# Infini-attention beside a SiLU feed-forward on one core: the bias of the turned heads made by VectorE, GpSimd's small scale operations planned at their real length, two buffers for memory's sums

## The chip, the core and the metric

The kernel runs on one core of one Trainium2 chip. The metric is the device time of one execution in microseconds, here the median of several runs; less is better. A core has five engines that run side by side, each with its own queue of instructions that it takes strictly in order: TensorE (PE in the profile, with its weight loads as PEld), VectorE (DVE), ScalarE (ACT), GpSimd (POOL) and SyncE (SP), which here issues most of the transfers. [...]

## The reference

The input has 2048 rows of 448 numbers. One branch is an attention with memory: 16 heads of 28, four segments of 512 rows; inside a segment a causal softmax attention, and beside it a retrieval from a matrix that sums the keys and values of all earlier segments. The other branch is a feed-forward layer, 448 to 1792 to 448, with SiLU. A gate mixes the two row by row.

```python
for s in range(N):                                   # 4 segments
    logits = jnp.einsum("bhqd,bhkd->bhqk", qs, ks) * scale + mask
    p = _softmax(logits, axis=-1)
    a_dot = jnp.einsum("bhqk,bhkd->bhqd", p, vs)
    pq = phi(qs)                                     # phi(t) = t + 1 if t > 0 else exp(t)
    num = jnp.einsum("bhld,bhde->bhle", pq, M)
    den = jnp.einsum("bhld,bhd->bhl", pq, z)[..., None] + 1e-6
    o = g * (num / den) + (1.0 - g) * a_dot
    pk = phi(ks)
    M = M + jnp.einsum("bhld,bhle->bhde", pk, vs)
    z = z + jnp.einsum("bhld->bhd", pk)
...
h = _silu(jnp.einsum("bsd,df->bsf", x, w1))
out = jnp.einsum("bsf,fd->bsd", h, w2)
return g * a + (1 - g) * b                           # g = sigmoid(x . gate_w)
```

## The kernel before

**Precision.** Almost every product is made of float16 pairs: an operand is split in a high part (made by ScalarE as a scaled copy) and the rest (made by VectorE or GpSimd), and TensorE multiplies high by high, high by low and low by high. The power-of-two scales for this are found on the chip from the sizes of the data. A few columns hold them (`top`, `up`), and GpSimd makes from them, in many operations on one to sixteen numbers per partition, every scale and bias that later instructions take as an operand. The helper `by` (L533, L535) issues these, in the functions `true`, `kscale`, `others` and `derive`.

**Stages.** In the first 180 us or so the projections run (`project`): x and the weights are loaded, split, multiplied to q, k, v and the gate (`product`, L637), and q, k and v are written to scratch memory in DRAM. In the same stage `memory` adds up phi(k) times v per segment and group of four heads: TensorE leaves the sum in PSUM, VectorE folds it into a buffer `md` (L1065), GpSimd masks it with `bds` (L1068) and adds it to `macc` (L1070), ScalarE and GpSimd split it again (L1073, L1074), and `retrieve` multiplies it with phi(q) (L1091 to L1106). From about 180 to 455 us the attention runs: 16 tiles (4 segments by 4 groups), each of four heads, between them the first pass of the feed-forward layer (10 of its 14 slices of 128) and part of the second. After that the second pass ends, with the output projection (`sc<-wos,oT`).

**Two kinds of heads.** Three of four heads of a tile (all four of the first tile) are computed with the keys along the partitions: their row maxima are found ahead of time in `maxima` (L744, L754), enter the product as two more rows, and ScalarE only takes exp (L1385). The fourth head of tiles 1 to 15, the *turned* one, has the queries along the partitions (`scores`, L1331 to L1345). Its four blocks of rows come in three groups, block 3 (512 wide), blocks 2 and 0 (384 and 128), block 1 (256). For each group TensorE multiplies (L1331), VectorE finds the maximum of each row in PSUM with the mask added (L1337; each block is one reduction and one short read of the accumulator), ScalarE turns each maximum into a bias, maximum times a scale plus a constant (L1341, the function `drop`), and takes exp with that bias (L1345). For every head ScalarE then makes the high half `phl` (L1398), GpSimd the low half in three pieces (L1402), and TensorE multiplies by v (L1421). A turned head's halves are transposed by two transfers first.

**What sets the order.** Nothing is ordered by hand. A small list scheduler in the kernel (`Sched`) takes tasks with an estimated length per engine (`act`, `dve`, `pool`, `few` and others put it there), dependencies, the buffers that they take and a priority, and plays the program forward on these estimates; the order in which it starts the tasks is the order of each engine's queue. Buffers are rings (`Ring`): a task that takes a buffer is started after the last user of the one before. So an estimate, a priority or the length of a ring that is changed anywhere can move instructions everywhere. The some 50 numbers at the top of the file (`TLEAD`, `PRICE`, `WOT` and so on) are priorities and costs of that scheduler.

`few(n, ...)` plans n of GpSimd's small operations at 0.33 us each. In `others`, the function `go` with `mem` issues six operations and `kscale` two before it, and `scores` seven.

Of the kernel before, what the change touches and what calls it, by code (L numbers as in the profile page):

```python
# [8 lines left out]
F32 = mybir.dt.float32  # L9
# [4 lines left out]
AF = mybir.ActivationFunctionType  # L14
OP = mybir.AluOpType
# [3 lines left out]
S, D, H, DH, NSEG, L, F = 2048, 448, 16, 28, 4, 512, 1792  # L19
NG = 4  # L20
GW = 4 * DH
# [8 lines left out]
TALL = 2.0 ** 15  # L30
NEG = -1.0e38
TURNED = 1
TLEAD = 41.9
TLOW = -26.78
TVP = 12.29
NTURN = 1
NT = NSEG * NG
NH = NT * 4
NA = 5
COLD = 5.0  # L40
WARM = 8
MORE = 6
HPRIO = 22.58
BANKS = {"mm": 3, "sc": 3, "cc": 2}
FREE = FB - 1
PASSES = [list(range(0, 10)), list(range(10, FB))]
# [3 lines left out]
DOWN = 2.0 ** -19  # L50
TINY = 2.0 ** -40
FIT = 2.0 ** -15
WOT = 269.88
TUS = 1.6
TLAT = 4.0
SLACK = -0.5
LOP = 63.28
LATE = -0.1
FIRST = 166.08
WPRIO = 65.13  # L60
MAXO = 60.98
FULL = 0.111
LOCK = 0.06
RB = "cc"
MP = 25.49
VF = -55.25
VA = 12.69
VS = 3.39
NV = 8
XH0 = -53.53  # L70
NF = 4
VE = 0.78
LASTQ = 6.05
WQS = -123.0
VH = 51.92
XS0 = -53.05
VC = -7.5
OT1 = -150.13
XS = 41.57
QS = -34.91  # L80
KS1 = -30.59
SS = -11.48


def VP(o, k):
    return o + VA + VS * k if o or k > VF else -1.0 + 0.1 * k


PRICE = 218.62
PRICE2 = 41.61  # L90
SLACK2 = 0.34
PVRUNS = [((1, 0), 1)]
PVP = 65.99
FLO = 52.62
FHI = 689.43
WOP = 107.76
SZ = 16.55
SZSTEP = 0.11
XPRIO = 368.0
WBP = 35.98  # L100
XLEAD = 146.82


# [180 lines left out]
def infini_mix(ctx: ExitStack, tc: tile.TileContext, x, wq, wk, wv, wo, beta, w1, w2, out):  # L284
    nc = tc.nc
# [50 lines left out]
    def act(cols, fn, *deps, **k):  # L336
        return sch.add("ACT", 0.06 + 0.00083 * cols, fn, deps, **k)
# [4 lines left out]
    def dve(cols, fn, *deps, **k):  # L342
        return sch.add("DVE", 0.07 + 0.00104 * cols, fn, deps, **k)
# [39 lines left out]
    WV, WQ, HQ, WK, HK, W1, W2, WO, NS = range(NSEG, NSEG + 9)  # L383
    cols, at = {}, 0
# [50 lines left out]
    SIZE, SQUARED, SCALED, XH, JUNK = {}, {}, {}, {}, []  # L435
# [85 lines left out]
    LATER, GDONE, QREADY, VREADY, END1 = [], [], {}, {}, []  # L521
# [34 lines left out]
    def others(s, prio, bds, own, t_own, t_gh):  # L556

        def mem():
            z = spk[:, NSEG + s:NSEG + s + 1]
            by(z, top[:, WK:WK + 1], top[:, xi(s)], 1.0 / FIT)  # L560
            by(z, z, 1.0 / UP, op0=OP.max)
            by(bds[:, s, :, DH:], own[:, :, None], z[:GW])
            by(bds[:, s, :, :DH], own[:, :, None].to_broadcast([GW, 4, DH]), z[:GW], rv[:GW, s:s + 1])

        def go():
            by(rv[:, s:s + 1], top[:, WV:WV + 1], top[:, xi(s)], 1.0 / FIT)
            by(omgs[:, s], omg, rv[:, s:s + 1])
            if s < NSEG - 1:
                mem()
        PREADY[s] = few(7 if s < NSEG - 1 else 2, go, SCALED[WV], SCALED[NSEG - 1 - s], KREADY.get(s), t_own, t_gh, prio=prio)  # L570

        def scores():
            x = top[:, xi(s)]
            by(es[:, NSEG:], top[:, WQ:WQ + 1], x, SCALE / FIT / FIT)
            by(es[:, s:s + 1], top[:, WK:WK + 1], x, es[:, NSEG:])
            by(es[:, s:s + 1], es[:, s:s + 1], 2.0 ** -100, op0=OP.max)
            by(nes[:, s:s + 1], es[:, s:s + 1], -1.0)
            for lo, j in ((0, WQ), (64, WK)):
                sl = slice(lo, lo + 64)
                by(wide[sl, s:s + 1], top[sl, j:j + 1], top[sl, xi(s)], 1.0 / FIT)  # L580
            by(wide[:, NSEG + s:NSEG + s + 1], wide[:, s:s + 1], 0.5)
        EREADY[s] = few(7, scores, PREADY[s], SCALED[WQ], SCALED[WK], prio=prio + 0.5)
        END1.append(EREADY[s])

    DER = {}
# [1 line left out]
    def derive(s, prio):  # L587

        def go():
            by(ths[:, s:s + 1], top[:, xi(s)], top[:, W1:W1 + 1], 0.5)  # L590
            by(hs[:, s:s + 1], up[:, xi(s)], up[:, W1:W1 + 1], DOWN)
            by(us[:, s:s + 1], ths[:, s:s + 1], top[:, W2:W2 + 1], 2.0 / DOWN)
            by(ogs[:, s * TB:s * TB + TB], ogate[:, s * TB:s * TB + TB], us[:, s:s + 1])
            by(hso[:, s:s + 1], wide[:, s:s + 1], hs[:, s:s + 1])
        return few(5, go, SCALED[W1], EREADY[s], GDONE[s], prio=prio)

    def rest(e, out, a, s, b):

# [175 lines left out]
    def project():  # L774
# [12 lines left out]
        def ring(name, shape, dt, n, tag=None):  # L787
            R[name] = tiles(wp, name, shape, dt, n, tag)
# [18 lines left out]
        def c1():  # L807
# [13 lines left out]
            t_wm, takes=[wb], prio=-200)  # L821
# [11 lines left out]
        def guards():  # L833
            for j in guard:
# [9 lines left out]
                       prio=50))  # L844
# [280 lines left out]
        t_gh = gates()  # L1125
# [13 lines left out]
        for t in range(NT):  # L1139
            s, g = divmod(t, NG)  # L1140
# [20 lines left out]
        for i, (j, src, n, how) in enumerate(pieces):  # L1161
            r, p = Buf(RAW), SZ + i * SZSTEP
# [156 lines left out]
    def scores(t, hh, rg, rs, pf, prio):  # L1319

        s, nb, ex = t // NG, Buf(C["nb"]), []
        for rows in ((3,), (2, 0), (1,)):
            ps = Buf(BK["sc"])
            at, n = [], 0
            for i in rows:
                at.append((i, n, n + 128 * (i + 1)))
                n = at[-1][2]

            def go(at=at, ps=ps):
                for i, lo, hi in at:  # L1330
                    nc.tensor.matmul(ps.v[:, lo:hi], rg.v[:KS, 0, hh, i * 128:(i + 1) * 128], rg.v[:KS, 1, hh, :hi - lo],  # L1331
                                     start=True, stop=True)

            def red(at=at, ps=ps):
                for i, lo, hi in at:
                    r = ps.v[:, lo:hi]
                    nc.vector.tensor_tensor_reduce(r, r, MK[:, L - (hi - lo):], 1.0, NEG, OP.add, OP.max, nb.v[:, 0, i:i + 1])  # L1337

            def drop(at=at):
                for i, lo, hi in at:  # L1340
                    nc.scalar.activation(nb.v[:, 1, i:i + 1], nb.v[:, 0, i:i + 1], AF.Identity, bias=lift, scale=nes[:, s:s + 1])  # L1341

            def exps(at=at, ps=ps):
                for i, lo, hi in at:
                    nc.scalar.activation(pf.v.rearrange("p b n -> p (b n)")[:, 64 * i * (i + 1):64 * (i + 1) * (i + 2)], ps.v[:, lo:hi],  # L1345
                                         AF.Exp, bias=nb.v[:, 1, i:i + 1], scale=es[:, s:s + 1])
# [107 lines left out]
    for c in range(NC + 1):  # L1454
        r = Buf(RAW)
# [121 lines left out]
```

## Time and profile before

| | |
|---|---|
| time, median of 3 runs | 558.37 us (557.99 to 558.53) |
| the profiled execution: its own time | 559.56 us |
| the profiled execution: its span, first to last instruction | 557.8 us |
| mean granted TensorE clock | 0.992 |
| TensorE matmul busy | 540.5 us (97%) |
| ScalarE busy | 428.0 us (77%) |
| VectorE busy | 400.1 us (72%) |
| GpSimd busy | 344.2 us (62%) |

One execution was profiled; it took 559.56 us, 1.19 us more than the median, and its span is 1.8 us shorter than its time. All windows and groups below are of this execution. In a row of a group stand the line of the kernel, the engine, the operation, output<-input with the shape (partitions x elements), the count, the busy time in us and the mean of one in ns, and after the bar the idle time just before, with what ended it. In a row of a timeline stand the start and the length in us. A matmul's end is modelled, so the matmul row counts some waiting as busy.

### The profile page before, as it was taken

What the parts mean: (1) busy time and instruction counts of PE and PEld (TensorE: products, weight loads), DVE (VectorE), ACT (ScalarE), POOL (GpSimd) and SP (SyncE); (2) the same over time, 40 slices, a digit from 0 to 9 for tenths busy, and PEclk for the clock granted to TensorE, in tenths of its full rate; (3) what the DMA queues carried; (4) which work ended last, traced back from release to release, by engine and by line L of the source; (5) the groups of instructions that cost most, each with busy time, mean ns of one, the idle gap of its engine ahead of it and who ended that gap; (6) DMA issues with size and microseconds to landing.
All of it is one profiled execution on the core that took longest, in us unless ns stands there. A gap on an engine that the chain in (4) does not pass through costs nothing.

```text
span 557.8 us, 11621 instructions
## 1 busy us (share of the span) xinstructions
PE 540.5 (97%) x3984; PEld 296.4 (53%) x3984; DVE 400.1 (72%) x1021; ACT 428.0 (77%) x771; POOL 344.2 (62%) x528
## 2 busy tenths in 40 slices
PE   8999999999999899999999999999899999999996
PEld 3445656566545465455565555555455545555543
DVE  4999989999677764887557778766677519663462
ACT  5979988756369988999889999989899897511140
POOL 3245555853415697679888789788789985212210
PEclk9999999999999999999999999999799999999999
DMA  8878866445485455427554276569613532789951
GB/s 277 257 229 273 244 195 192 154 141 142 137 224 137 107 158 149 113 71 165 134 130 117 83 170 166 127 171 204 99 27 94 129 83 71 249 229 243 247 157 67
DMA packets 117240, 88.72 MB, mean 159 GB/s; under 512 B 83348, under 2 KB 106900, under 8 KB 117180
## 3 DMA queue, kind: packets, MB, share of 16 engines
q1 hardware_dynamic: 116604, 86.99, 58.2%
q10 hardware_dynamic: 576, 0.99, 0.5%
q8 instruction: 31, 0.51, 0.4%
q14 instruction: 29, 0.24, 0.1%
HBM read 48.38 MB, written 26.06 MB: 133 GB/s over the span
## 4 chain that ended last, share of the span: by engine, by line
PE 57%; ACT 26%; POOL 6%; DVE 4%; issue 4%; DMA 2%; SPq 0%; DVEq 0%; ACTq 0%
PE mm L637 14%; PE mm L1243 13%; PE sc L637 9%; ACT phl L1398 5%; ACT pf L1385 5%; PE cc L1243 5%; PE cc L637 4%; ACT pf L1345 4%; PE sc L744 3%; PE sc L1380 3%; PE cc L1421 3%; ACT th L1220 2%; ACT nb L1341 2%; POOL phl L1402 2%; DMA xraw<-in_x_dram 1%
## 5 line engine op out<-in xcount | busy, mean ns | idle before, releaser
L1402 POOL TENSOR_TENSOR phl<-pf,phl 128x384 f16<-128x384 f32 (+1 forms) x192 | 188.0, 1002 | 40.5 <-ACT phl L1398 40.5
L1243 PE MATMUL mm<-wb,ghl 128*128 128x448 f16 (+2 forms) x516 | 109.7, 348 | 0.0
L637 PE MATMUL mm<-xh,wa 128*128 128x512 f16 x429 | 106.7, 379 | 0.0
L754 DVE CUSTOM_DVE_ANT_0 sc<-sc,mk 128x256 f32<-128x256 f32 (+2 forms) x147 | 81.2, 568 | 30.5 <-PE sc L744 25.9
L1385 ACT ACTIVATE pf<-sc,lift,es 128x512 f32<-128x512 f32 x147 | 96.8, 719 | 6.2 <-PE sc L1380 6.0
L1243 PEld LDWEIGHTS <-ghl 128*128 128x128 f16 x684 | 64.2, 97 | 53.5 <-issue 2.4
L637 PEld LDWEIGHTS <-wa 128*128 128x128 f16 x572 | 54.5, 98 | 57.6 <-issue 4.5
L1398 ACT ACTIVATE phl<-pf 128x1280 f16<-128x1280 f32 x64 | 81.5, 1278 | 4.2 <-POOL pf L1392 3.6
L744 PE MATMUL sc<-ring 84*128 84x384 f16 (+2 forms) x196 | 47.6, 301 | 3.9 <-ACT pf L1345 2.0
L1380 PE MATMUL sc<-ring 86*128 86x512 f16 x196 | 45.8, 302 | 4.8 <-ACT pf L1385 3.1
L648 POOL TENSOR_TENSOR ol<-ol,ml 128x448 f32<-128x448 f32 x12 | 13.7, 1140 | 50.1 <-DMA ol<-o_scr 27.5
L637 PE MATMUL mm<-xh,wks 128*128 128x512 f16 x176 | 42.7, 379 | 0.2 <-ACT pp L960 0.2
L637 PE MATMUL mm<-xh,wqs 128*128 128x512 f16 x176 | 42.0, 380 | 0.3 <-ACT pp L960 0.2
L1429 DVE TENSOR_REDUCE oraw<-cc 128x116 f32<-128x232 f32 x64 | 25.2, 394 | 23.2 <-PE cc L1421 22.8
L1421 PEld LDWEIGHTS <-phl 128*128 128x128 f16 x980 | 32.4, 96 | 11.5 <-issue 4.2
L1243 PE MATMUL cc<-wb,ghl 128*128 128x448 f16 x168 | 38.1, 352 | 0.0
L637 PE MATMUL cc<-xh,wa 128*128 128x512 f16 x143 | 37.7, 395 | 0.2 <-DVE ghl L1226 0.2
L1220 ACT ACTIVATE th<-mm,ths 128x512 f32<-128x512 f32 x39 | 27.0, 696 | 12.2 <-PE mm L637 10.6
L1345 ACT ACTIVATE pf<-sc,nb,es 128x512 f32<-128x512 f32 (+3 forms) x60 | 35.1, 611 | 1.4
L637 PE MATMUL sc<-wos,oT 128*128 128x448 f16 x176 | 35.4, 353 | 0.0
L1226 DVE SCALAR_TENSOR_TENSOR ghl<-mm,ghl 128x512 f16<-128x512 f32 x39 | 26.6, 685 | 12.1 <-ACT ghl L1224 12.0
L1421 PE MATMUL cc<-vg,phl 128*128 128x29 f16 (+1 forms) x980 | 33.9, 183 | 0.3 <-POOL phl L1402 0.3
(202 smaller groups left out, 1018.5 us busy)
## 6 DMA issues: line engine op xcount, KB each, us to landing
rawf<-in_w_dram SPq DMA_DIRECT2D x26, 256.0 KB
rawf<-in_w_dram SPq DMA_DIRECT2D x28, 224.0 KB
v_scr<-vt SPq DMA_DIRECT2D x16, 232.0 KB
vg<-v_scr SPq DMA_DIRECT2D x16, 232.0 KB
xraw<-in_x_dram SPq DMA_DIRECT2D x14, 256.0 KB
q_scr<-stg SPq DMA_DIRECT2D x16, 224.0 KB
k_scr<-stg SPq DMA_DIRECT2D x16, 224.0 KB
ring<-q_scr SPq DMA_DIRECT2D x16, 224.0 KB
```

Source lines behind the costliest of these rows:

```text
L637: nc.tensor.matmul(ps(), *p[i], start=(i == 0), stop=(i == n - 1))
L744: nc.tensor.matmul(ps.v[:, u:u + n], rg.v[:KS, 0, hh, i * 128:(i + 1) * 128], rg.v[:KS, 1, hh, :n], start=(i > 0), stop=(i > 0 or j == nh ...
L754: nc.vector.tensor_tensor_reduce(r, r, MK[:, L - n:], 1.0, NEG, OP.add, OP.max, mx.v[:, hh, i:i + 1])
L1220: e1 = sact(L, lambda ps=ps, th=th: nc.scalar.activation(th.v, ps.v, AF.Tanh, scale=ths[:, s:s + 1]), m, takes=[th], uses=[ps], prio=p0)
L1226: e4 = dve(L, lambda ps=ps, g=g: nc.vector.scalar_tensor_tensor(g.v[:, 1], ps.v, DOWN, g.v[:, 0], op0=OP.mult, op1=OP.subtract), e3, uses= ...
L1243: nc.tensor.matmul(ps.v[:, lo:hi], g.v[:, y, sl], w.v[:, z, lo:hi], start=(j == 0 and i == 0), stop=(j == len(fs) - 1 and i == 2))
L1345: nc.scalar.activation(pf.v.rearrange("p b n -> p (b n)")[:, 64 * i * (i + 1):64 * (i + 1) * (i + 2)], ps.v[:, lo:hi], AF.Exp, bias=nb.v[: ...
L1380: nc.tensor.matmul(ps.v[:, e:e + w], rg.v[:KK, 1, hh, j * 128:(j + 1) * 128], rg.v[:KK, 0, hh, j * 128:], start=True, stop=True)
L1385: ex.append(sact(e, lambda b=b, ps=ps, pf=pf, e=e: nc.scalar.activation(pf.v[:, b, :e], ps.v[:, :e], AF.Exp, bias=lift, scale=es[:, s:s + ...
L1398: hi = copy(1280, lambda hl=hl, flat=flat: nc.scalar.activation(hl.v[:, 0], flat(), AF.Copy), *mk, takes=[hl], uses=[pf], prio=p0 + 2)
L1402: low = pool(w - u + 22, lambda hl=hl, flat=flat, u=u, w=w: nc.gpsimd.tensor_sub(hl.v[:, 1, u:w], flat()[:, u:w], hl.v[:, 0, u:w]), low, u ...
L1421: nc.tensor.matmul(p[:, i, :2 - z], hl.v[:, z, u:u + 128], vg.v[:, j, hh, :2 - z], start=(z == zs[0] and i == 0), stop=(z == zs[-1] and j ...
```

## The change

Four things change together.

1. In `scores` the function `drop` on ScalarE is gone. VectorE makes the bias itself, in the same task as the maxima, once per group instead of once per block: three instructions per turned head on one, two and one columns, in place of ScalarE's four. The task waits for the scale column `nes` (the task `EREADY[s]`), as the task on ScalarE did, and the exp waits for the maxima's task directly. The planned length of the maxima's task grows by 140 columns.
2. `few` is given larger numbers in three places: 11 and 3 for 7 and 2, 10 for 7, 6 for 5.
3. The ring `md`, the buffer of memory's sums, has two buffers instead of one.
4. The scheduler's numbers are other numbers. One of them, `MORE`, is also a count: of warm-up matmuls on zeros near the start, 4 instead of 6.

```diff
-TLEAD = 41.9
-TLOW = -26.78
+TLEAD = 49.11
+TLOW = -747.95
...
-MORE = 6
+MORE = 4
...
-        PREADY[s] = few(7 if s < NSEG - 1 else 2, go, SCALED[WV], SCALED[NSEG - 1 - s], KREADY.get(s), t_own, t_gh, prio=prio)
+        PREADY[s] = few(11 if s < NSEG - 1 else 3, go, SCALED[WV], SCALED[NSEG - 1 - s], KREADY.get(s), t_own, t_gh, prio=prio)
...
-        EREADY[s] = few(7, scores, PREADY[s], SCALED[WQ], SCALED[WK], prio=prio + 0.5)
+        EREADY[s] = few(10, scores, PREADY[s], SCALED[WQ], SCALED[WK], prio=prio + 0.5)
...
-        return few(5, go, SCALED[W1], EREADY[s], GDONE[s], prio=prio)
+        return few(6, go, SCALED[W1], EREADY[s], GDONE[s], prio=prio)
...
-        ring("md", [GW, 4, DH + 1], F32, 1)
+        ring("md", [GW, 4, DH + 1], F32, 2)
...
-            def drop(at=at):
-                for i, lo, hi in at:
-                    nc.scalar.activation(nb.v[:, 1, i:i + 1], nb.v[:, 0, i:i + 1], AF.Identity, bias=lift, scale=nes[:, s:s + 1])
+                rows = slice(at[-1][0], at[0][0] + 1, 2)
+                nc.vector.tensor_scalar(nb.v[:, 1, rows], nb.v[:, 0, rows], nes[:, s:s + 1], lift, op0=OP.mult, op1=OP.add)
...
-            r = dve(n + 184 * len(at), red, m, takes=[] if ex else [nb], uses=[ps, nb], prio=prio)
-            d = act(150 * len(at), drop, r, EREADY[s], uses=[nb], prio=prio)
-            ex.append(act(n + 180 * len(at) - 70, exps, d, takes=[] if ex else [pf], uses=[ps, pf, nb], prio=prio))
+            r = dve(n + 184 * len(at) + 140, red, m, EREADY[s], takes=[] if ex else [nb], uses=[ps, nb], prio=prio)
+            ex.append(act(n + 180 * len(at) - 70, exps, r, takes=[] if ex else [pf], uses=[ps, pf, nb], prio=prio))
```

Because the whole plan is played again, the order of every engine's queue differs almost from the start. Three places are shown, in rows of the engine's queue: line, operation, output<-input, shape, and a count where equal rows follow each other. In the changed file the lines behind `scores` are three lower, so the exp of a turned head is L1343 there and L1345 before.

ScalarE at the first turned head (`pf` takes the exp, `nb` holds maxima and biases, `phl` is the high half of a head, `wb` a weight of the feed-forward layer). Before:

```order
L1398 ACTIVATE phl<-pf 128x1280
L611 ACTIVATE wb<-rawf,up 128x448 x2
L1341 ACTIVATE nb<-nb,lift,nes 128x1
L1345 ACTIVATE pf<-sc_2515,nb,es 128x512
L1341 ACTIVATE nb<-nb,lift,nes 128x1 x2
L1345 ACTIVATE pf<-sc_2518,nb,es 128x384
L1345 ACTIVATE pf<-sc_2518,nb,es 128x128
L1341 ACTIVATE nb<-nb,lift,nes 128x1
L1345 ACTIVATE pf<-sc_2522,nb,es 128x256
```

The same place in the change:

```order
L1395 ACTIVATE phl<-pf 128x1280
L611 ACTIVATE wb<-rawf,up 128x448
L1343 ACTIVATE pf<-sc_2479,nb,es 128x512
L611 ACTIVATE wb<-rawf,up 128x448
L1343 ACTIVATE pf<-sc_2483,nb,es 128x384
L1343 ACTIVATE pf<-sc_2483,nb,es 128x128
L1343 ACTIVATE pf<-sc_2507,nb,es 128x256
```

The four small instructions are gone from ScalarE's queue, here and at the other 14 turned heads (679 rows of the queue become 643). In 11 of the 15 heads the four exps now stand directly behind one another; in four, something else stands between the first and the second.

VectorE at the same head, in the change (ISA rows are the masked reduction and the read of its accumulator):

```order
L1337 ISA sc_2479,nb<-sc_2479,mk 128x512
L1337 ISA nb 128x1
L1339 TENSOR_SCALAR nb<-nb,nes,lift 128x1
L1337 ISA sc_2483,nb<-sc_2483,mk 128x384
L1337 ISA nb 128x1
L1337 ISA sc_2483,nb<-sc_2483,mk 128x128
L1337 ISA nb 128x1
L1339 TENSOR_SCALAR nb<-nb,nes,lift 128x2
L1337 ISA sc_2507,nb<-sc_2507,mk 128x256
L1337 ISA nb 128x1
L1339 TENSOR_SCALAR nb<-nb,nes,lift 128x1
```

The three new instructions stand directly behind the maxima that they read; the second works on two columns. Before, the eight L1337 rows stood behind one another without them.

GpSimd in the first segment, where the small scale operations (`bds`, then `es`) meet memory's sums (`macc<-md,bds`), as a piece of the difference:

```order
 L533 TENSOR_SCALAR bds<-of,spk 112x4
 L535 TENSOR_SCALAR bds<-of,spk,rv 112x4x28
+L1068 TENSOR_TENSOR macc<-md,bds 112x116
 L535 TENSOR_SCALAR es<-top 128x1
 L535 TENSOR_SCALAR es<-top,es 128x1
```

The first sum is now taken before the scales of the scores, where it stood behind them.

More of the change, by code (lines that the diff above doesn't have):

```diff
@@ L32 @@
 TURNED = 1
-TLEAD = 41.9
-TLOW = -26.78
-TVP = 12.29
+TLEAD = 49.11
+TLOW = -747.95
+TVP = -51.66
 NTURN = 1
@@ L41 @@
 WARM = 8
-MORE = 6
-HPRIO = 22.58
+MORE = 4
+HPRIO = 27.62
 BANKS = {"mm": 3, "sc": 3, "cc": 2}
@@ L52 @@
 FIT = 2.0 ** -15
-WOT = 269.88
+WOT = 284.64
 TUS = 1.6
@@ L56 @@
 SLACK = -0.5
[L57 to L61, printed above, removed]
+LOP = 88.06
+LATE = -0.12
+FIRST = 168.71
+WPRIO = 17.7
+MAXO = 61.09
 FULL = 0.111
@@ L64 @@
 RB = "cc"
[L65 to L68, printed above, removed]
+MP = 24.27
+VF = -52.84
+VA = 11.23
+VS = 1.35
 NV = 8
-XH0 = -53.53
+XH0 = -76.85
 NF = 4
[L72 to L76, printed above, removed]
-VC = -7.5
[L78 to L82, printed above, removed]
+VE = 1.05
+LASTQ = 6.73
+WQS = -115.94
+VH = 30.5
+XS0 = -41.95
+VC = -7.5
+OT1 = -137.97
+XS = 35.3
+QS = -33.19
+KS1 = -25.27
+SS = -12.61
 def VP(o, k):
     return o + VA + VS * k if o or k > VF else -1.0 + 0.1 * k
-PRICE = 218.62
-PRICE2 = 41.61
-SLACK2 = 0.34
+PRICE = 266.2
+PRICE2 = 94.57
+SLACK2 = -0.63
 PVRUNS = [((1, 0), 1)]
[L93 to L100, printed above, removed]
+PVP = 65.05
+FLO = 23.74
+FHI = 670.43
+WOP = 63.38
+SZ = 14.98
+SZSTEP = 0.06
+XPRIO = 345.58
+WBP = 34.14
 XLEAD = 146.82
```

## The prediction

> **What bounds the kernel now.** I read the page first: the span, the busy shares, the chain that ended last by engine.
>
> ```profile
> span 557.8 us, 11621 instructions
> PE 540.5 (97%) x3984; PEld 296.4 (53%) x3984; DVE 400.1 (72%) x1021; ACT 428.0 (77%) x771; POOL 344.2 (62%) x528
> PE 57%; ACT 26%; POOL 6%; DVE 4%; issue 4%; DMA 2%; SPq 0%; DVEq 0%; ACTq 0%
> ```
>
> TensorE is busy nearly all the time, but the chain runs through ScalarE for a quarter of the span, so TensorE is not the only bound. Where the two meet shows when the span is cut at the kernel's own stages. The columns are engine by engine the busy time in the window; then the granted clock, the transfer share and GB/s.
>
> ```profile
> 0.00:180.00 180.00, 176.87 (x969) 96.25 (x970) 152.32 (x348) 134.61 (x291) 86.33 (x195) 1.00 0.67 201
> 180.00:455.00 275.00, 265.50 (x2436) 149.63 (x2434) 188.20 (x571) 258.50 (x428) 230.32 (x306) 0.99 0.52 125
> 455.00:558.00 103.00, 98.18 (x583) 50.50 (x581) 59.53 (x103) 34.86 (x56) 27.51 (x29) 0.99 0.63 176
> ```
>
> The first row is the projections, the second the attention, the third the end. In the first and the third ScalarE has room. In the attention it is busy 258.50 of 275 us (94%) beside a TensorE that is busy 265.50: two engines, each nearly full, whose work hangs on each other's. VectorE has 275 - 188.20 = 86.80 us to spare there. TensorE stands still for 275 - 265.50 = 9.50 us in this stage, and 180 - 176.87 = 3.13 us in the first.
>
> The chain of waits, cut to the attention, by line:
>
> ```profile
> by line: PE mm L1243 17.4%; ACT phl L1398 10.3%; ACT pf L1385 10.2%; ACT pf L1345 7.8%; PE cc L1243 6.4%; PE sc L1380 5.3%; PE sc L744 5.0%; PE cc L1421 4.6%; issue 4.6%; ACT th L1220 4.5%; ACT nb L1341 4.2%; POOL phl L1402 3.7%; PE cc L637
> ```
>
> The ScalarE lines that are listed make 37.0% (10.3 + 10.2 + 7.8 + 4.5 + 4.2), and L1341, the bias, 4.2% of 275 us = 11.55 us. That is the line that the change takes away.
>
> **The bias leaves ScalarE.** The group of L1341 in the attention, and one turned head on the two engines:
>
> ```profile
> L1341 ACT ACTIVATE nb<-nb,lift,nes 128x1 f32<-128x1 f32 x60 | 21.2, 378 | 1.1 <-DVE nb L1337 0.9
> ```
>
> ```profile
> 315.09 0.67 ACT L1220 ACTIVATE th<-mm,ths 128x512 f32<-128x512 f32 x1
> 315.65 0.37 ACT L1341 ACTIVATE nb<-nb,lift,nes 128x1 f32<-128x1 f32 x1
> 316.06 0.78 ACT L1345 ACTIVATE pf<-sc,nb,es 128x512 f32<-128x512 f32 x1
> 316.74 0.65 ACT L1341 ACTIVATE nb<-nb,lift,nes 128x1 f32<-128x1 f32 x2
> 317.29 1.00 ACT L1345 ACTIVATE pf<-sc,nb,es 128x384 f32<-128x384 f32 x2
> 318.19 0.38 ACT L1341 ACTIVATE nb<-nb,lift,nes 128x1 f32<-128x1 f32 x1
> ```
>
> ```profile
> 315.01 0.14 DVE L1337 DVE_READ_ACCUMULATOR2_ANT nb<- 128x1 f32 x1
> 315.52 0.14 DVE L1337 DVE_READ_ACCUMULATOR2_ANT nb<- 128x1 f32 x1
> 315.92 0.14 DVE L1337 DVE_READ_ACCUMULATOR2_ANT nb<- 128x1 f32 x1
> 316.30 0.14 DVE L1337 DVE_READ_ACCUMULATOR2_ANT nb<- 128x1 f32 x1
> ```
>
> Four of them per head, 15 heads: 60 instructions, 21.2 us. ScalarE waits for VectorE hardly at all (0.9 us in three cases): in the head shown the last maximum is read at 316.44, when ScalarE has just begun the first exp. So the biases cost ScalarE's own time, and its load in the attention falls from 258.50 to 237.3 us, 86% of the stage.
>
> In their place VectorE gets three instructions per head, 45 in all. Their price is not in a row of this kind; the nearest are four of the same operation with a scale from a column:
>
> ```profile
> 351.69 0.21 DVE L1462 TENSOR_SCALAR os<-os,up 128x1 f32<-128x1 f32 x1
> 351.82 0.20 DVE L1463 TENSOR_SCALAR os<-os,top 128x1 f32<-128x1 f32 x1
> 352.06 0.21 DVE L1464 TENSOR_SCALAR os<-os,top 128x1 f32<-128x1 f32 x1
> 352.31 0.69 DVE L1465 TENSOR_SCALAR gas<-gate,os 128x16 f32<-128x16 f32 x1
> 348.95 4.89 POOL L1402 TENSOR_TENSOR phl<-pf,phl 128x512 f16<-128x512 f32 x5
> ```
>
> At 0.21 us it is 45 x 0.21 = 9.5 us more for VectorE, beside 86.80 us of room: no cost by its load. The 0.69 us of the fourth is taken up below.
>
> How much of the 21.2 us reaches the end? From above: not more than the 11.55 us that the chain holds of L1341, and unless TensorE also has waiting hidden inside its modelled busy time, not more than the 9.50 us for which it stands still. From below: if each head's bias stays on the chain and only moves to VectorE, the chain keeps 15 x 3 x 0.21 = 9.5 of its 11.55 us and 2.1 us are won; and nothing at all if TensorE's own queue sets the pace throughout. I take 5.0 us, half of the 9.50: the chain's listed lines in the attention are about as much TensorE's (17.4 + 6.4 + 5.3 + 5.0 + 4.6 = 38.7%) as ScalarE's (37.0%), and a shorter ScalarE helps only where ScalarE leads. Part of TensorE's time it can't give back in any case: its clock.
>
> ```profile
> 360.00:400.00 40.00, 37.51 (x347) 20.86 (x346) 28.31 (x85) 38.45 (x64) 34.45 (x48) 0.94 0.78 167
> 400.00:440.00 40.00, 39.36 (x348) 22.06 (x347) 27.59 (x80) 36.87 (x61) 34.84 (x44) 0.97 0.37 82
> ```
>
> With clocks of 0.94 and 0.97, 2.4 + 1.2 = 3.6 us of these 80 go to the clock; I leave them where they are.
>
> Where the stall goes: with ScalarE lighter, the next to be late at a turned head is VectorE itself, whose three new instructions stand between the maxima. In the change's order a `phl` stands ahead of the first exp at all 15 heads (directly at 14, with half of a weight between at the first), which gives VectorE a start.
>
> ```profile
> L1398 ACT ACTIVATE phl<-pf 128x1280 f16<-128x1280 f32 x60 | 76.4, 1277 | 4.2 <-POOL pf L1392 3.6
> ```
>
> Its 1.277 us is more than the 3 x 0.21 us that VectorE adds per head. This cover gone, those heads would give back 0.63 us each, which is the lower of the two cases above.
>
> **The second buffer of memory's sums.** The waits of those who use `md`:
>
> ```profile
> L1065 DVE TENSOR_REDUCE md<-cc x12: 330/390/400, 45.3 to 140.0; 112x116 f32<-112x232 f32 x12
>   DVE md L1065: 11.3, 6
>   POOL macc L1068: 0.4, 1
> ```
>
> A single buffer makes VectorE's fold wait for GpSimd; it did so once, for 0.4 us. The 11.3 us are GpSimd waiting for VectorE, which a buffer does not change. Gain between 0 and 0.4 us, 3.13 us of TensorE's standing still being all there is in that stage; I take 0.
>
> **GpSimd's planned lengths and the new numbers.** No instruction becomes longer or shorter by them; they only order the queues anew. GpSimd is busy 86.33 of the first 180 us, and the small operations are a part of that. Two of them:
>
> ```profile
> L533 POOL TENSOR_SCALAR omgs<-omg,rv 128x16 f32<-128x16 f32 x4 | 3.0, 744 | 7.0 <-DVE omg L920 6.7
> L535 POOL TENSOR_SCALAR rv<-top 128x1 f32<-128x1 f32 x4 | 2.6, 655 | 0.0
> ```
>
> At 744 and 655 ns these were twice the 0.33 us that the plan gave them, so the plan comes nearer to the chip, and memory's first sum is taken ahead of the scores' scales, which no exp needs before the attention. The reordering could win at most the 3.13 us of the first stage; what it can lose no row bounds, and I put it at as much again. I take 0. The end I leave as it is: TensorE is busy for 98.18 of its 103 us. A handful of splits and sums also pass from GpSimd to VectorE, which idles for 557.8 - 400.1 = 157.7 us; I count them as nothing.
>
> **Two warm-up matmuls less.** They stand ahead of the first projection:
>
> ```profile
> 20.48 1.04 PE L824 MATMUL mm<-maskb 128*128 128x512 bf16 x4
> 19.26 2.56 ACT L611 ACTIVATE wqs<-raw,up 128x512 f16<-128x512 f32 x4
> 21.36 0.38 PE L637 MATMUL mm<-xh,wqs 128*128 128x512 f16 x1
> ```
>
> The weights' high parts end at 21.82, and the projection needs them; the matmuls on zeros fill the wait. Removing two of four is worth nothing, at most half of 21.36 - 20.48, 0.4 us.
>
> **The sum.** 559.56 us of the profiled execution - 5.0 (ScalarE's relief) - 0 - 0 - 0 = 554.56. The profiled execution lay 559.56 - 558.37 = 1.19 us above the median, so the median after is 553.4 us.
>
> **The rivals.**
>
> *More is won.* If the whole 9.50 us of TensorE's standing still in the attention goes, 558.37 - 9.50 = 548.9 us. For it: ScalarE at 94% is the fuller partner when TensorE's queue waits. Against it: GpSimd, at 230.32 of 275 us, stays as it was, and the chain's POOL and issue parts with it. Chance 0.12.
>
> *Nothing is won.* TensorE is the only pace, ScalarE's relief turns into idle time of ScalarE: 558.4 us. For it: 97% busy, and an end where it is alone. Against it: 37.0% of the attention's chain on ScalarE. Chance 0.11.
>
> *The second bias waits for GpSimd: slower.* The row of L1465 above took 0.69 us where its neighbours took 0.21, while GpSimd was inside a train of `phl` pieces. Three neighbours on one column ran during the same train without loss; the one on 16 columns lost 0.69 - 0.21 = 0.48 us. The change's second bias works on two columns. If it is held in the same way, 15 x 0.48 = 7.2 us fall on the path between the first and the second exp, for in 11 heads nothing stands between them: 558.37 - 5.0 + 7.2 = 560.6 us. It decides from 5.0 / 15 = 0.33 us of holding per head. Against it: the first exp runs 0.78 us meanwhile, and VectorE may be ahead by the `phl`. Chance 0.13. [...]
>
> *The new order loses elsewhere: slower.* All queues are reordered. If TensorE's 3.13 us of standing still in the first stage become three times as much (6.3 us more), the sum is 558.37 - 5.0 + 6.3 = 559.7 us. For it: single waits there are long (6.7 us ahead of `omgs` in the row above), so a chain that slips by one can cost microseconds. Against it: the plan now knows GpSimd's real lengths in just this stage. It decides from 5.0 us. Chance 0.12.
>
> That the change does not do what it says can be left out: the four instructions are gone from ScalarE's queue at all 15 heads.
>
> **How the numbers follow.** The forecast has 0.52, the rivals 0.12, 0.11, 0.13 and 0.12. Below 0.2% (1.1 us, about what a measurement of this kernel can tell from no change) counts as the same. Faster: 0.52 + 0.12 = 0.64; same: 0.11; slower: 0.13 + 0.12 = 0.25. The forecast alone runs from 551.2 us (558.37 - 7.1, three quarters of the 9.50) to 556.3 (558.37 - 2.1). For eight in ten the range takes in most of the larger gain and both slower cases: 548 to 561 us.
>
> **What would show it.** Right: no L1341; ScalarE busy near 237 us in the attention and TensorE standing still there for about 5 us; the attention some 5 us shorter, with the first 180 and the last 103 us as they were; new VectorE rows of about 0.2 us; the chain with less ScalarE and more TensorE. The third rival shows as two-column rows of 0.5 us or more and as exps (384 wide) that wait for VectorE; the fourth as a first stage that is longer. The forecast is wrong if the attention keeps its 275 us although ScalarE is lighter, or if the gain comes from the first or last stage.

## The result and the profile after

The change takes 552.45 us (median of 4 runs, 550.76 to 552.75), beside 558.45 us for the kernel before in runs of the same chip. The ratio is 0.988, with a 95% interval of 0.9848 to 0.9911: 6.0 us gained. The forecast was 553.4 us.

The head of the page after: span, busy shares, the chain by engine.

```profile
span 550.4 us, 11586 instructions
PE 537.1 (98%) x3982; PEld 296.1 (54%) x3982; DVE 422.1 (77%) x1071; ACT 411.4 (75%) x712; POOL 337.6 (61%) x518
PE 61%; DVE 14%; ACT 13%; DMA 5%; issue 3%; POOL 3%; DVEq 0%; ACTq 0%; SPq 0%; POOLq 0%
```

ScalarE lost 16.6 us of busy time (428.0 to 411.4) and half of its share of the chain (26% to 13%); VectorE gained 22.0 us and 10 points of the chain. Where the time went shows best when the span is cut at two events that both kernels have, the first and the last `phl` on ScalarE (a head's high half). First the kernel before, then the change; the columns are the window, its length, then PE, PEld, DVE, ACT and POOL busy with their counts, the granted clock, the transfer share and GB/s.

```profile
0.00:171.30 171.30, 168.17 (x904) 91.49 (x905) 146.16 (x334) 125.91 (x278) 80.72 (x187) 1.00 0.67 203
171.30:459.90 288.60, 279.10 (x2523) 156.61 (x2522) 195.60 (x587) 271.92 (x448) 240.78 (x320) 0.99 0.53 126
459.90:557.80 97.90, 93.28 (x560) 48.28 (x558) 58.30 (x102) 30.14 (x49) 22.64 (x22) 0.99 0.64 180
```

```profile
0.00:170.50 170.50, 167.28 (x900) 91.45 (x901) 146.71 (x333) 125.79 (x278) 79.61 (x185) 1.00 0.69 204
170.50:455.50 285.00, 279.19 (x2557) 157.87 (x2556) 217.25 (x639) 257.26 (x390) 237.77 (x315) 0.99 0.55 129
455.50:550.40 94.90, 90.62 (x531) 46.74 (x527) 58.10 (x101) 28.37 (x46) 20.23 (x19) 0.99 0.64 181
```

Of the 7.4 us of span, 0.8 come from the projections, 3.6 from the attention, 3.0 from the end. (One execution each: in four executions whose projections have the same order, those of the kernel before and of three experiments below, this stage took 170.2 to 173.5 us, so the 0.8 us say nothing.) The end is not faster; it has less to do: 531 products where there were 560, and the attention does 34 more (2557 for 2523). So the attention is shorter and holds more of the feed-forward work. TensorE stands still there for 285.00 - 279.19 = 5.81 us, before for 9.50.

The new instructions, by form (count, busy us, mean ns):

```profile
L1339 DVE TENSOR_SCALAR nb<-nb,nes,lift 128x1 f32<-128x1 f32 x30 | 8.2, 273 | 1.1
L1339 DVE TENSOR_SCALAR nb<-nb,nes,lift 128x2 f32<-128x2 f32 x15 | 10.2, 683 | 0.5
```

and who waited for them, from the list of waits (us in total, times, longest):

```profile
ACT pf L1343 <- DVE nb L1339: 3.7, 7, 1.0
```

One element more per partition, and the instruction is two and a half times as long in the mean (683 ns for 273). The timeline says why: VectorE (rows 1 and 2) and GpSimd (row 3) at one head, then the same two engines at another.

```profile
278.30 0.75 DVE L1339 TENSOR_SCALAR nb<-nb,nes,lift 128x2 f32<-128x2 f32 x1
278.96 0.42 DVE L1337 CUSTOM_DVE_ANT_0 sc<-sc,mk 128x256 f32<-128x256 f32 x1
278.10 2.03 POOL L1399 TENSOR_TENSOR phl<-pf,phl 128x384 f16<-128x384 f32 x2 [0.50 <-ACT phl L1395]
...
260.30 0.29 DVE L1339 TENSOR_SCALAR nb<-nb,nes,lift 128x2 f32<-128x2 f32 x1
260.52 0.92 POOL L1399 TENSOR_TENSOR phl<-pf,phl 128x384 f16<-128x384 f32 x1 [1.34 <-ACT phl L1395]
```

At 278.30 GpSimd had just begun a piece of 0.92 us; the two-column bias ended at 279.05, with that piece. At 260.30 GpSimd was idle, and the same instruction took 0.29 us. It is so at all 15 heads: four two-column biases took 0.29 us, and each of the other eleven ended 0.02 to 0.03 us behind the end of a piece of GpSimd's. The 30 one-column biases took 0.272 to 0.274 us, although 22 of them ran wholly inside such a piece. In the trace the two-column biases wait for a semaphore of VectorE's own alone, and the train at 278.10 us waits for ScalarE (the 0.50 us of its row): no semaphore stands between the two instructions, and one held up the other all the same. The holding that the third rival named is there. What it costs, the experiments show.

### The profile page after: what moved, and what is told of

Same layout as the page of the kernel before. It is cut to its first block, busy times and chain, and to the rows that moved or that the text cites. A ratio compares the mean times of both kernels' runs of the same rounds, so it can differ in the third digit from the quotient of the medians.

```text
span 550.4 us, 11586 instructions
## 1 busy us (share of the span) xinstructions
PE 537.1 (98%) x3982; PEld 296.1 (54%) x3982; DVE 422.1 (77%) x1071; ACT 411.4 (75%) x712; POOL 337.6 (61%) x518
## 4 chain that ended last, share of the span: by engine, by line
PE 61%; DVE 14%; ACT 13%; DMA 5%; issue 3%; POOL 3%; DVEq 0%; ACTq 0%; SPq 0%; POOLq 0%
PE mm L1243 15%; PE mm L637 12%; PE sc L637 8%; PE cc L1243 6%; ACT pf L1382 4%; PE cc L637 4%; PE sc L744 4%; PE cc L1418 4%; PE sc L1377 3%; DMA rawf<-in_w_dram 3%; ACT phl L1395 3%; PE sc L1000 2%; DVE sc L1337 2%; DVE stg L942 1%; DVE nb L1339 1%
## 5 line engine op out<-in xcount | busy, mean ns | idle before, releaser
L1243 PE MATMUL mm<-wb,ghl 128*128 128x448 f16 (+2 forms) x516 | 112.3, 350 | 0.0
L1377 PE MATMUL sc<-ring 86*128 86x512 f16 x196 | 48.0, 305 | 0.5 <-DVE mx L754 0.4
L654 ACT ACTIVATE oh<-ol,os 128x448 f16<-128x448 f32 x16 | 10.6, 662 | 37.4 <-POOL ol L648 37.4
L1343 ACT ACTIVATE pf<-sc,nb,es 128x512 f32<-128x512 f32 (+3 forms) x60 | 33.3, 608 | 3.9 <-DVE nb L1339 3.7
L1337 DVE CUSTOM_DVE_ANT_0 sc<-sc,mk 128x512 f32<-128x512 f32 (+3 forms) x60 | 29.4, 491 | 3.8 <-PE sc L1331 2.9
```

The lines of the kernel that those rows point to most:

```text
L1243: nc.tensor.matmul(ps.v[:, lo:hi], g.v[:, y, sl], w.v[:, z, lo:hi], start=(j == 0 and i == 0), stop=(j == len(fs) - 1 and i == 2))
L1377: nc.tensor.matmul(ps.v[:, e:e + w], rg.v[:KK, 1, hh, j * 128:(j + 1) * 128], rg.v[:KK, 0, hh, j * 128:], start=True, stop=True)
```

## The experiments

All ratios are to the kernel before on the same chip in the same session, with 95% intervals. The runs fall into two kinds. In the first the scheduler plays the same plan and only instructions are exchanged, so that every other instruction stays where it was. In the second the plan is played again.

| run | bias by | order of the queues | median us | ratio |
|---|---|---|---|---|
| before | ScalarE | old | 558.45 to 559.59 by session | 1 |
| old_order_vector_bias | VectorE, two columns | old | 556.71 | 0.9957 (0.9936 to 0.9978) |
| old_order_one_column | VectorE, one column | old | 550.92 | 0.9840 (0.9815 to 0.9864) |
| new_order_scalar_bias | ScalarE | new | 562.99 | 1.0082 (1.0054 to 1.0109) |
| the change | VectorE, two columns | new | 552.45 | 0.9880 (0.9848 to 0.9911) |
| one_column_bias | VectorE, one column | new | 548.22 | 0.9813 (0.9789 to 0.9837) |

### The bias on VectorE in the old order

```diff
+                rows = slice(at[-1][0], at[0][0] + 1, 2)
+                nc.vector.tensor_scalar(nb.v[:, 1, rows], nb.v[:, 0, rows], nes[:, s:s + 1], lift, op0=OP.mult, op1=OP.add)
...
-            def drop(at=at):
-                for i, lo, hi in at:
-                    nc.scalar.activation(nb.v[:, 1, i:i + 1], nb.v[:, 0, i:i + 1], AF.Identity, bias=lift, scale=nes[:, s:s + 1])
+            def drop():
+                pass
```

> The queues of before, instruction for instruction, but the 60 ScalarE biases are taken out and the 45 VectorE ones stand behind their maxima (the plan is not played again). Theory 'relief' (the gain comes from ScalarE's 21.2 us whatever the order): 553.5 to 555.5 us. Rival 'order' (the gain comes from the new order of the queues): no lower than 557.5 us.

556.71 us, a ratio of 0.9957: 2.2 us below before (558.93), less than the one theory asked for and more than the other allowed. Something takes most of the relief back. The list of waits names it:

```profile
ACT pf L1346 <- DVE nb L1339: 13.5, 20, 2.0
```

and the list by form gives its size:

```profile
L1339 DVE TENSOR_SCALAR nb<-nb,nes,lift 128x2 f32<-128x2 f32 x15 | 12.5, 830 | 0.5
```

ScalarE waits for a bias for 13.5 us in 20 cases, and the two-column bias takes 0.830 us in the mean. In the new order it takes 0.683 us, with 3.7 us of waiting; beside the 0.29 us of one that is not held the mean is longer by 0.54 us here and by 0.39 us there. The attention, cut as above:

```profile
170.20:456.20 286.00, 274.99 (x2524) 154.54 (x2522) 212.06 (x632) 254.91 (x387) 241.44 (x320) 1.00 0.53 127
```

TensorE stands still for 286.00 - 274.99 = 11.01 us, more than the 9.50 before. The stage is shorter only because TensorE's busy time is, at a granted clock of 1.00 for 0.99. The clocks of the single runs say the same: seven runs at 0.999 or 1.000 took 554.64 to 557.01 us; the four at 0.996 or 0.997 took 557.31 to 558.85, beside 557.21 to 559.66 for the kernel before at 0.995 to 0.997 in that session. At like clocks no gain is left that can be told; why this program is more often granted the full clock is open.

### The bias back on ScalarE in the new order

```diff
-                rows = slice(at[-1][0], at[0][0] + 1, 2)
-                nc.vector.tensor_scalar(nb.v[:, 1, rows], nb.v[:, 0, rows], nes[:, s:s + 1], lift, op0=OP.mult, op1=OP.add)
...
             def exps(at=at, ps=ps):
+                for i, lo, hi in at:
+                    nc.scalar.activation(nb.v[:, 1, i:i + 1], nb.v[:, 0, i:i + 1], AF.Identity, bias=lift, scale=nes[:, s:s + 1])
```

> The queues of the change, instruction for instruction, but the bias is made by ScalarE again, right ahead of the exps of its group (60 instructions back on ScalarE, 45 off VectorE, the plan not played again). 'Relief': 557 us or more, since the 21 us come back onto ScalarE and the order has no place for them. 'Order': no higher than 554.5 us.

562.99 us, 1.0082. "Relief" holds and "order" falls: with the same queues, ScalarE's biases cost 1.0082 - 0.9880 = 0.020 of the time, 11 us. This order was planned for a ScalarE without them, so part of that is the misfit. The attention, cut as above:

```profile
170.10:466.10 296.00, 281.23 (x2557) 157.99 (x2556) 204.23 (x594) 275.90 (x450) 238.10 (x316) 0.99 0.52 124
```

The same 2557 products take 296.00 us instead of 285.00, TensorE stands still for 14.77 us, and ScalarE is busy for 275.90.

### One column at a time

```diff
-                rows = slice(at[-1][0], at[0][0] + 1, 2)
-                nc.vector.tensor_scalar(nb.v[:, 1, rows], nb.v[:, 0, rows], nes[:, s:s + 1], lift, op0=OP.mult, op1=OP.add)
+                for i, lo, hi in at:
+                    nc.vector.tensor_scalar(nb.v[:, 1, i:i + 1], nb.v[:, 0, i:i + 1], nes[:, s:s + 1], lift, op0=OP.mult, op1=OP.add)
```

> The change with the bias of the second group made by two instructions on one column each in place of one on two columns; nothing else, the plan not played again. Theory 'lock' (a two-column bias is held by GpSimd's work, a one-column one is not): the two take 0.55 us together where the one took 0.68, ScalarE's wait for the bias (3.7 us) falls below 2.5 us, and the time is 0 to 2 us below the change's. Rival 'two columns are simply dear' (no holding): the two take as long as or longer than the one, the wait stays, time the same or up to 1 us more.

548.22 us, 0.9813, though VectorE issues 15 instructions more. The holding is gone: the 60 biases took 0.270 us in the mean, as the 30 on one column did in the change (0.273 us); two take 0.54 us where the one took 0.683, and the list of waits has no entry of ScalarE for a bias left. Four microseconds fall, twice the upper end of what was expected. The list by form:

```profile
L1339 DVE TENSOR_SCALAR nb<-nb,nes,lift 128x1 f32<-128x1 f32 x60 | 15.0, 270 | 1.1
```

and the attention, cut as above:

```profile
169.40:450.80 281.40, 276.91 (x2557) 157.66 (x2555) 212.19 (x654) 256.23 (x390) 237.98 (x315) 0.99 0.56 131
```

The attention is 3.6 us shorter with the same 2557 products. The projections are 1.1 us shorter, within their spread between executions, and the end is as long as in the change. This version beats both kernels.

The same edit in the old order, on the first experiment's kernel:

> The queues of before with the bias made by VectorE, as in the run with the old order before, but every bias on one column (60 instructions). Theory 'lock': the second bias no longer waits for GpSimd, so of that run's 13.5 us in which ScalarE waits for a bias some 6 us go, and the time is 552 to 555 us, 2 to 4 us below that run. Rival 'late by its place' (the old order gives VectorE's bias no head start, lock or not): ScalarE's wait stays above 10 us and the time within 1 us of that run (0.9957 of before).

550.92 us, 0.9840, 5.8 us below the run with two columns (6.5 us by the ratios, since the sessions differ), by more than expected (2 to 4 us). ScalarE's wait for the biases falls from 13.5 to 5.0 us, 8.5 us less where some 6 were expected (list of waits):

```profile
ACT pf L1346 <- DVE nb L1339: 5.0, 15, 0.8
```

The attention, cut as above:

```profile
173.50:453.50 280.00, 274.01 (x2523) 154.83 (x2522) 205.13 (x647) 254.68 (x388) 241.60 (x320) 1.00 0.55 130
```

With the old order's 2523 products the attention takes 280.00 us, 8.6 less than before. TensorE stands still for 5.99 us of it, 3.5 less than before; the other 5.1 us are in its busy time (274.01 for 279.10). The clock is not what makes this gain: at 0.996 or 0.997 four runs took 548.64 to 551.67 us, where the kernel before, at 0.995 to 0.997 in that session, took 558.62 to 561.40. So the relief of ScalarE by itself, free of the holding, is worth 0.016 of the time in the old order, 8.9 us.

### The numbers, the lengths, the buffer

In the runs of this part the plan is played again, but for one. With the new numbers alone, the lengths alone and the second buffer alone a planning step was added, which takes the buffer of the transposed halves for whichever transfer comes first; added to the kernel before, or to the change, it leaves every queue as it was.

```diff
+                room = sch.add("SP", 0.0, lambda: None, [hi], takes=[pr], uses=[hl], prio=p0)
...
-                    pr.v[:, z].rearrange("p (b q) -> p b q", b=10), hl.v[:, z]), [d], takes=[] if z else [pr], uses=[hl, pr],
+                    pr.v[:, z].rearrange("p (b q) -> p b q", b=10), hl.v[:, z]), [d, room], uses=[hl, pr],
```

Before with all the new numbers:

```diff
-TLEAD = 41.9
+TLEAD = 49.11
...
-MORE = 6
+MORE = 4
...
```

> Before with the scheduler's new numbers only (warm-ups included): ScalarE makes the biases, small operations at their old planned length, one buffer of sums; the plan is played again. 'Relief': 556 to 560 us, since ScalarE keeps its 21.2 us. 'Order': 552 to 554.5 us.

569.21 us, 1.0172 (1.0152 to 1.0193). Worse than either theory said. The numbers bring nothing by themselves.

The change with all the old numbers:

```diff
-TLEAD = 49.11
+TLEAD = 41.9
...
```

> The change's code (VectorE's bias on two columns, real lengths, two buffers) planned with the scheduler's old numbers. Theory 'relief': the code alone gains, 554 to 557 us. Rival 'numbers fit the code' (the new numbers were needed to keep the plan good): 559 us or more.

561.22 us, 1.0018 (0.9995 to 1.0042). The code alone, replayed, gains nothing; the rival holds.

Before with the bias alone, as the change has it:

```diff
-            r = dve(n + 184 * len(at), red, m, takes=[] if ex else [nb], uses=[ps, nb], prio=prio)
-            d = act(150 * len(at), drop, r, EREADY[s], uses=[nb], prio=prio)
...
+            r = dve(n + 184 * len(at) + 140, red, m, EREADY[s], takes=[] if ex else [nb], uses=[ps, nb], prio=prio)
```

> Before with the change of the bias alone, in the change's own form (two columns, the planner told of the longer task on VectorE), the plan played again with the old numbers; lengths and buffers as before. 'Relief' and a neutral replay: 555 to 558 us (the old order with the bias on VectorE gave 0.9957 of before). If any replay with the old numbers loses: 560 us or more, as with lengths or buffer alone.

558.70 us, 0.9990 (0.9974 to 1.0007), a little above the first range and below the second; no gain that can be told.

Before with the real lengths alone:

```diff
-        PREADY[s] = few(7 if s < NSEG - 1 else 2, go, SCALED[WV], SCALED[NSEG - 1 - s], KREADY.get(s), t_own, t_gh, prio=prio)
+        PREADY[s] = few(11 if s < NSEG - 1 else 3, go, SCALED[WV], SCALED[NSEG - 1 - s], KREADY.get(s), t_own, t_gh, prio=prio)
...
```

> Before with the small scale operations planned at the new lengths, nothing else; the plan is played again with the old numbers (a planning step of zero length settles who takes the buffer of the transposed halves first; alone it leaves every queue as it was). If the plan only gains in truth: 557 to 559 us. Rival 'any replay with numbers that were fitted to another plan loses': 560 us or more, with the loss in the attention and not in the first 180 us where the operations stand.

575.58 us, 1.0285 (1.0255 to 1.0314).

Before with the second buffer alone:

```diff
-        ring("md", [GW, 4, DH + 1], F32, 1)
+        ring("md", [GW, 4, DH + 1], F32, 2)
```

> Before with two buffers for memory's sums, nothing else; the plan is played again with the old numbers (with the same planning step of zero length). The one wait that the buffer removes is 0.4 us, so by itself 558.0 to 558.6 us. By the rival 'any replay loses': 560 us or more, with the loss in the attention.

577.19 us, 1.0319 (1.0296 to 1.0342). Both lie far above the 560 us at which the rival's range began, and only part of the loss is where the rival had it. The three stages of the last one:

```profile
0.00:172.50 172.50, 167.74 (x902) 91.39 (x903) 147.69 (x334) 125.36 (x278) 81.21 (x187) 1.00 0.68 202
172.50:466.00 293.50, 276.56 (x2471) 153.81 (x2470) 196.06 (x585) 268.94 (x442) 242.28 (x319) 0.96 0.51 121
466.00:575.90 109.90, 104.47 (x614) 53.45 (x612) 62.70 (x104) 34.17 (x54) 23.52 (x22) 1.00 0.58 166
```

The attention is 4.9 us longer although it does 52 products fewer (2471 for 2523), and these are done afterwards: the end has 614 products for 560 and is 12.0 us longer. The granted clock in the attention is 0.96, for 0.99 before. Three windows within it show where it is low:

```profile
200.00:210.00 10.00, 10.00 (x104) 6.02 (x102) 7.39 (x25) 9.74 (x17) 9.83 (x12) 1.00 0.64 164
210.00:220.00 10.00, 6.56 (x71) 3.46 (x68) 5.34 (x17) 8.57 (x13) 8.85 (x14) 0.88 0.63 138
220.00:230.00 10.00, 8.58 (x74) 4.58 (x73) 8.06 (x24) 5.89 (x10) 9.13 (x10) 0.50 0.42 102
```

TensorE first stands still for 3.44 of 10 us, its queue waiting mostly for ScalarE's exps and GpSimd's `phl`; then its clock is at half (0.50 in 220 to 230 us). Here time goes twice, in the waiting and in the low clock behind it; that the one brings the other is not shown.

Before with the second buffer on the chip alone, unknown to the planner:

```diff
-        ring("md", [GW, 4, DH + 1], F32, 1)
+        R["md"] = Ring(1, lambda: wp.tile([GW, 4, DH + 1], F32, name="md", tag="md", bufs=2))
```

> Before with a second buffer for memory's sums on the chip, while the planner still counts one: every queue stands as before, instruction for instruction, and only VectorE's wait for the buffer (0.4 us) is gone. By the prediction's step: 0 to 0.4 us below before. If the buffer itself does harm (the rival to 'any replay loses' for the run with the second buffer only): 2 us or more above before.

558.42 us, 0.9983 (0.9966 to 1.0000). The buffer itself does no harm; it is worth at most a fraction of a per cent, as the single 0.4 us wait said, and that wait is gone from the list. The 3% above were the plan.

The change with one buffer:

```diff
-        ring("md", [GW, 4, DH + 1], F32, 2)
+        ring("md", [GW, 4, DH + 1], F32, 1)
```

> The change with one buffer for memory's sums, the plan played again with the new numbers. The buffer by itself: at most 0.4 us, 552 to 553 us. If only the fit of numbers and plan matters: 554 to 562 us, lost in the attention.

554.77 us, 0.9923 (0.9902 to 0.9944), some 2.3 us above the change. The intervals overlap, but the six runs (553.89 to 555.97 us) all lie above the change's four (550.76 to 552.75). The loss is not in the attention (284.10 us):

```profile
0.00:174.50 174.50, 168.42 (x900) 90.96 (x901) 145.22 (x331) 126.77 (x280) 82.27 (x185) 1.00 0.67 199
174.50:458.60 284.10, 278.11 (x2557) 157.38 (x2556) 217.10 (x639) 257.05 (x391) 237.47 (x315) 0.99 0.55 129
```

In the profiled execution it is in the projections, 174.50 us for 170.50, where the sums stand; one execution of a stage that varies by some 3 us does not prove the place. The buffer by itself was to be worth 0.4 us at most, and that fails; the other half of the expectation has the time right (554 to 562 us) and the place wrong. With the new numbers the order seems to lean on the second buffer.

The change with the small operations planned at the old lengths:

```diff
-        PREADY[s] = few(11 if s < NSEG - 1 else 3, go, SCALED[WV], SCALED[NSEG - 1 - s], KREADY.get(s), t_own, t_gh, prio=prio)
+        PREADY[s] = few(7 if s < NSEG - 1 else 2, go, SCALED[WV], SCALED[NSEG - 1 - s], KREADY.get(s), t_own, t_gh, prio=prio)
...
```

> The change with the small operations planned at the old lengths, the plan played again with the new numbers. If the real lengths themselves matter on the chip, the loss lies in the first 180 us; if only the fit of numbers and plan matters, it lies in the attention: 554 to 562 us.

552.74 us, 0.9879 (0.9855 to 0.9903), just below the range expected and no different from the change. The real lengths do nothing that can be measured in the final plan.

## Why the prediction was right, and where not

**The bound and the direction** were right: two nearly full engines in the attention, and ScalarE the one to relieve. The runs with exchanged instructions show it without the plan's part: 0.0160 of the time in the old order (1 against 0.9840), 8.9 us. In the new order it is 0.0269 (1.0082 against 0.9813), 15.0 us, but there the biases stand in an order made without them.

**The main term, 5.0 us, was too small, and another was missing.** "Half of the 9.50" undersold the relief: in the old order it is 8.9 us, near the upper ends that were named (9.50 and 11.55). Against it stands a loss that the sum had at nothing, the holding of the two-column bias: 0.0067 in the new order (0.9880 against 0.9813), 3.7 us, and 0.0117 in the old one, 6.5 us. The net came out close to 5.0 because the two errors have opposite signs. That closeness is luck.

**TensorE's standing still was the wrong measure.** In the old order it fell by only 3.5 us while the attention lost 8.6, and with the two-column bias it grew to 11.01 us. The prediction's own reservation, waiting hidden inside the modelled busy time, is a likely reason beside the clock; it was not tested.

**ScalarE's load** was to fall by 21.2 us, to 237.3. With the order kept it fell by 17.0 in the attention (271.92 to 254.91), and in the prediction's window from 180 to 455 us the change shows 247.26. The rows of the biases overlap those beside them: the pair at 316.74 us begins before the first exp has ended and ends after the next has begun. So ScalarE gains less without them than the 21.2 us that they are busy.

**The third rival** had a chance of 0.13 and is at work, inside a gain. It had 0.48 us of holding per head; the change shows 0.683 - 0.29 = 0.39 us in the mean. It put the whole of it on the path, 7.2 us; the cost is about half of that, 3.7 us. That the `phl` and the first exp cover part, as the prediction's argument against it said, fits the 3.7 us for which ScalarE still waits. In the old order, where ScalarE waits 13.5 us, the holding took 6.5 of the 8.9 us.

**The other rivals.** The fourth did not come: in the first stage TensorE stands still for 170.50 - 167.28 = 3.22 us, before for 3.13. The first had 548.9 us, which the change does not reach; with one column it is 548.22 us.

**VectorE's price** was 0.21 us per instruction and is 0.273 on one column: the 45 instructions cost 18.4 us, not 9.5. The rows that were taken as nearest have one scale column, the bias has two columns as operands. The kernel before has a row of that kind:

```profile
L497 DVE TENSOR_SCALAR most<-sizes,top,most 128x1 f32<-128x1 f32 x2 | 0.5, 272 | 0.0
```

The room of 86.80 us held it.

**"The next to be late is VectorE itself"** was right: its share of the chain went from 4 to 14%.

**The clock** was wrong as a step: 3.6 us "it can't give back in any case". In the kernel before, TensorE stood still for 1.95 us of 392 to 396 us and was then at half clock; in the change the low stretch lies elsewhere (0.51 in 184 to 188 us).

```profile
392.00:396.00 4.00, 2.05 (x27) 1.20 (x27) 3.82 (x10) 3.97 (x7) 3.82 (x4) 0.90 0.54 68
396.00:400.00 4.00, 4.00 (x31) 2.13 (x30) 1.98 (x5) 4.00 (x7) 3.50 (x7) 0.50 0.95 155
```

In the old order with VectorE's bias, on two columns and on one, the profiled executions show 1.00 in the attention. So some of the clock's time can be had. For the one-column bias it is a small part of the gain, as the runs at like clocks show; the small gain of two columns in the old order is seen only in the runs at 0.999 or 1.000.

**The end** was to stay as it was, and the prediction named a gain from the first or last stage as a sign of being wrong. By length, 3.0 us come from the end. The counts show why this is not another mechanism: 29 products fewer stand behind the last `phl` and 34 more ahead of it, in the attention. The prediction looked at the length of the stage and not at what the lighter attention would draw in. TensorE's standing still in the attention, forecast at about 5 us, is 5.81.

**The second buffer and the lengths at nothing**: right for the buffer in the old order (0.9983) and for the lengths in the new plan (0.9879 against 0.9880). What was missing is that the new plan seems to rest on the second buffer, about 2 us. The lengths were also misread: 744 and 655 ns are means of very unequal rows. The four `rv` took 0.26 to 1.39 us and the four `omgs` 0.34 to 1.42 us, so the shortest took about what the plan gave them, 0.33 us. The longest `rv` (from 42.55 us) ended 0.05 us behind one of VectorE's `xh` instructions, which would fit the same holding the other way round; it is one row, and no run tested it.

**The new numbers at nothing** was right as a net, but not as the reason given. They are not a gain and not idle either. With ScalarE's bias the new order is worse than the old (1.0082), with VectorE's two-column bias it is better (0.9880 against 0.9957), with one column nearly the same (0.9813 against 0.9840, intervals that overlap). In the new order ScalarE waits 3.7 instead of 13.5 us for the two-column bias; that this head start is the whole difference was not tested.

Not settled: why the replays with the lengths alone and with the second buffer alone make TensorE wait so long near 210 us. Which of the scheduler's choices does it was not tried. The two warm-up matmuls less were not tried by themselves either.

## What to carry to other kernels

Before an operation is moved to another engine, look for rows of the same operation on that engine while its neighbour works: one row of 0.69 us beside three of 0.21 announced the cost that took back a third of what was to be had (3.7 of 10.4 us). When a kernel's order comes from tuned numbers, an edit that is replayed without new numbers measures the plan along with the edit (the bias alone: 0.9990; the second buffer alone: 1.0319, in the old order 0.9983); exchange instructions in a fixed order to see the edit itself. And a stage that gets lighter draws work in from the next: count the products per stage, not only its length.

## What the runs showed of the hardware

**The `tensor_scalar` on two columns was held by GpSimd, the one on one column was not.** In the change four of the 15 on two columns took 0.29 us (at 260.30 us GpSimd was idle as it began), and each of the other eleven lasted up to the end of a piece of GpSimd's and 0.02 to 0.03 us more; the mean is 0.683 us, in the old order 0.830 us. The 30 on one column took 0.272 to 0.274 us, 22 of them wholly inside a piece. With all 60 on one column the mean is 0.270 us in both orders.

**TensorE's clock fell to one half behind some stretches in which it waited**, and stayed there for some microseconds: 0.50 from 395.2 to 402.0 us before, behind 1.63 us of standing still in 390 to 395.1 us, and 0.50 in 220 to 230 us with the second buffer only, behind 3.44 us of standing still in 210 to 220 us. It did not fall behind every such stretch: before, TensorE was busy for only 2.51 us of 184 to 188 us, and the clock stayed at 1.00. The 3.44 us are a sum of several gaps, the longest of 1.24 us. What sets the clock back is not shown.

**The same program was granted different clocks in different executions.** Of the twelve runs with the second buffer in the old order, the two with a mean clock of 1.000 took 555.9 us, the four with 0.990 took 558.2 to 559.6. The clock does not set the time alone: two others took 560.1 us at 0.994 and 559.2 us at 0.997.
